# Fewer, larger loads at the end of a decode block: W1 in two, W2 in four, the last V in three

## The chip, the cores and the metric

The kernel runs on one core of a Trainium2 chip. Its engines work side by side, each through its own list of instructions in order: PE (matrix products, with its weight loads shown apart as PEld), DVE (vector operations), ACT (activation functions), POOL, and SP, which here does nothing but issue loads. Data moves between the chip's main memory and the core's on-chip memory on 16 DMA engines. The metric is the time of one execution in microseconds on the device. The kernel before takes 1312.82 us, the median of three runs (1312.65 to 1312.91).

## The reference

One token for each of two sequences (B = 2) goes through an attention block with cached keys and values, and then through a two-layer MLP. All arrays are 32-bit floats.

```python
h  = x + softmax((LN(x) @ wq) . K^T * Dh**-0.5) . V @ wo     # 32 heads, 8192 keys, Dh = 128, D = 512
y  = LN(LN(h))
h2 = h + gelu(y @ w1 + b1) @ w2 + b2                         # w1: 512 x 1792, w2: 1792 x 512
```

K and V have 2 x 32 x 8192 x 128 numbers each, 268 MB apiece, and each number is used once. W1 and W2 have 3.67 MB each.

## The kernel before

**Main loop.** A step `i` (0 to 31, `NI` = 32) is one sequence and one pair of heads. Its K tile and its V tile are 128 partitions x 128 keys x 128 numbers, 64 KB in each partition and 8.39 MB in all: partitions 0 to 63 hold one head, 64 to 127 the other. They lie in a pool of three buffers (`kv`, `BUFS = 3`), so a load waits until the tile that had its buffer three loads earlier is used up. DVE multiplies K by q in four chunks (`multiply`, L220), DVE and ACT sum over the 128 numbers (L228, L224), the maximum and the exponentials follow (`row_max`, `all_max`, `exps`), and PE multiplies the exponentials with V: `values` (L280), 32 groups `u` of four keys of each partition; each group is one product, which the trace shows as two instructions. The result lies in PSUM (`so`); ACT copies it out (`gather`, L286), and PE sums it over partitions (`head_sum`, L301, and L294 for the last two steps).

**Loads.** SP issues nearly all of them, in program order. Step 31's V, `vt[31]` (L354), is loaded in four pieces, by keys of a partition: 0-63, 64-95, 96-119 and 120-127. Behind it come four small loads of b1 and b2 (L359, L360), then W1 in four loads of 128 rows each (L415, one row of 7 KB for each partition, `c` counting the loads), then W2 in six (L419), of 4, 4, 2, 2, 1 and 1 rows of 2 KB for each partition. W1 and W2 share one tile `ws` of the pool `kv`, in the buffer that step 31's K had.

**The end, from L411 on.** Only products of step 31 and the MLP are left. PE's order there is written out by hand: `behind(last)` puts the instructions in its block after `last`. The order is: `values` of the last V for groups 0-15; `head_end` of step 30 (L294, then DVE's L423); 4 products of nothing that keep PE running (`keep_warm`, L461); groups 16-23; `into`, which starts two sums in PSUM with the residual rows (L470); 8 of `keep_warm`; groups 24-29 and 30-31; `keep_warm`; `head_end` of step 31. Group `u` reads keys 4u to 4u+3, so groups 0-15 need the first V piece, 16-23 the second, 24-29 the third, 30-31 the fourth.

Then `project` multiplies by the last rows of wo twice (L477): into `hc`, which holds h with its mean taken out, and into `po2`, which holds h + b2. `hc` has column block `n` (128 of the 512 columns of h) in partitions 32n and 32n+1. DVE copies it (L504), PE turns it (L509), and the result `cen` has column 128n + p of h in partition p. It is multiplied with W1 (L520; W1's row 128c + p lies in partition p), the variance comes from L526 and L528, then follow the scale and b1 (L536), gelu (L538, ACT), a turn in 32 x 32 blocks (L540, DVE), W2 in 14 products `t` of four blocks each (L543), a copy (L546) and the store (L548).

Of the kernel before, what the change touches and what calls it, by code (L numbers as in the profile page):

```python
# [16 lines left out]
P = 128  # L17
# [5 lines left out]
NG = 4  # L23
# [9 lines left out]
def tile_decode_block(ctx: ExitStack, tc: tile.TileContext, x, k, v, wq, wo, w1, b1, w2, b2, out):  # L33
    nc = tc.nc
    B, H, SK, DH = k.shape
# [5 lines left out]
    DC = D // P  # L41
# [19 lines left out]
    def load(src, i, parts):  # L61
        m, b = divmod(i, B)
        t = kv.tile([P, NS, DH], F32, name="kv", tag="kv")
        rows = src[b, QG * m:QG * m + QG].rearrange("h (p j) d -> (h p) j d", j=NS)
        for s0, n in parts:
            nc.sync.dma_start(t[:, s0:s0 + n], rows[:, s0:s0 + n])
        return t
# [4 lines left out]
    ident = const.tile([P, P], F32, name="ident")  # L72
# [88 lines left out]
    otl = const.tile([P, QG, B], F32, name="otl")  # L161
# [51 lines left out]
    wl = q2.rearrange("p (e n) -> p e n", e=QG)  # L213

    def multiply(i, c):
        if c == 0:
            ST[i] = work.tile([P, NS], F32, name="s", bufs=3)
        qb = qps[i // B][:, i % B, None, :].to_broadcast([P, CH, DH])
        kc = kt[i][:, c * CH:(c + 1) * CH, :]
        return nc.vector.tensor_tensor(kc, kc, qb, op=ALU.mult)  # L220

    def by_act(i, c):
        for j in range((c + 1) * CH - NACT[c], (c + 1) * CH):
            nc.scalar.activation(kt[i][:, j, :], kt[i][:, j, :], AF.Copy, accum_out=ST[i][:, j:j + 1])  # L224
# [12 lines left out]
    def all_max(i):  # L237
        gm = work.tile([1, QG], F32, name="gm")
        last = nc.vector.tensor_reduce(gm, MT.pop(i).rearrange("o (e p) -> o e p", e=QG), axis=AX.X, op=ALU.max,  # L239
                                       negate=True)  # L240
        GM[i] = psm.tile([P, 1], F32, name="sm")
        for e in range(QG):
            nc.tensor.matmul(GM[i][e * HP:(e + 1) * HP], srow, gm[:, e:e + 1], start=True, stop=True)  # L243
        return last

    def exps(i):
        m, b = divmod(i, B)
        nb = work.tile([P, 1], F32, name="nb")
        nc.scalar.activation(nb, GM.pop(i), AF.Copy)  # L249
        if b == 0:  # L250
            LT[m] = work.tile([P, B], F32, name="ls")
        s = ST.pop(i).rearrange("p (u j) -> p u j", j=4)
        for e in range(QG):
            ps = slice(e * HP, (e + 1) * HP)
            nc.scalar.activation(ptz[i % 2][ps, :, 4 * e:4 * e + 4], s[ps], AF.Exp, bias=nb[ps], scale=SCALE,  # L255
                                 accum_out=LT[m][ps, b:b + 1])
# [19 lines left out]
    def values(i, us=range(NS // 4)):  # L276
        so = so2[i % 2]
        for u in us:
            n = u % NG
            m = nc.tensor.matmul(so[32 * n:32 * n + 4 * QG], ptz[i % 2][:, u, :], vt[i][:, 4 * u:4 * u + 4, :],  # L280
                                 start=(u < NG), stop=(u >= NS // 4 - NG))
        return m
# [52 lines left out]
    def behind(m):  # L335
        return tc.issue_after(m.ins)

    def cut(n):
        return [(j * NS // n, NS // n) for j in range(n)]

    parts_of = {NI - 3: cut(2), NI - 2: cut(4), NI - 1: cut(2)}
    kt, vt = {}, {}
# [3 lines left out]
    for i in range(NI):  # L346
        m, b = divmod(i, B)
        done = i - 1
        late = i == NI - 1
        if not late:  # L350
            if i < NI - 2:
                vt[i] = load(v, i, cut(1))
        else:
            vt[i] = load(v, i, [(0, 64), (64, 32), (96, 24), (120, 8)])  # L354
            b1r = rows2[:, 0].rearrange("p r q -> p (r q)")[:, :FN]
            nc.vector.memset(b1r, 0.0)
            b2s = rows2[:B, 1].rearrange("b r q -> b (r q)")
            for e in range(B):
                nc.sync.dma_start(b1r[e::32], b1.rearrange("(n f) -> n f", n=NG))  # L359
                nc.sync.dma_start(b2s[e:e + 1], b2[None, :])  # L360
        if i > 0:
            last = all_max(done)
            exps(done)
            if not late:
                values(done)
        if i < NI - 1:
            kt[i + 1] = load(k, i + 1, parts_of.get(i + 1, cut(1)))
        if i == NI - 2:
            vt[i] = load(v, i, cut(1))
            nc.sync.dma_start(wl, wo[HL * DH:, :].rearrange("(h p) n -> p h n", p=P))  # L370
        if next_load < len(groups) and i == free_from:
            load_wo(next_load, MX[i - 1][:1, 0:1] if next_load == 0 else None)
            next_load += 1
            free_from = NI
        for c in range(NC):
            if i > 0 and c == 0:
                with behind(last):
                    mul = multiply(i, c)
            else:
                mul = multiply(i, c)  # L380
            ended = [g for g in group_end.get(done // B, ())] if done >= 0 and done % B == B - 1 else []
            with behind(mul):
                if i > 0 and c == 1:
                    inverse(done)
                if i > 0 and c == 2 and done % B == B - 1:
                    for h in range(done // B * QG, done // B * QG + QG):
                        head_out(h)
                if c == 3:
                    for g in ended:
                        turned(g)  # L390
                        free_from = i + 1
            by_act(i, c)
            if i > 0 and c == 0 and not late:
                gather(done)
            by_dve(i, c)
            if i > 0 and c == 0:
                total(done)
            if i > 0 and c == 1 and not late:
                head_sum(done)
            if c == 2:  # L400
                for g in ended:
                    turn(g)
        if b == B - 1 and m + 1 < NM:
            make_q(m + 1)
        if late:
            with behind(values(done, range(MOST))):
                row_max(i)
        else:
            row_max(i)
# [1 line left out]
    hl = NI - 1  # L411
    wt = kv.tile([P, 2, NS * DH // 2], F32, name="ws", tag="kv")
    w1t = wt[:, 0, :DC * F].rearrange("p (c f) -> p c f", c=DC)
    for c in range(DC):
        nc.sync.dma_start(w1t[:, c], w1[c * P:(c + 1) * P])  # L415
    w2v = w2.rearrange("(p t) d -> p t d", t=FT)
    w2t = wt[:, 1, :FT * D].rearrange("p (t d) -> p t d", t=FT)
    for t, n in ((0, 4), (4, 4), (8, 2), (10, 2), (12, 1), (13, 1)):
        nc.sync.dma_start(w2t[:, t:t + n, :], w2v[:, t:t + n, :])  # L419

    def head_end(i):
# [3 lines left out]
    last = all_max(hl)  # L425
# [5 lines left out]
    with behind(last):  # L431
        last = values(hl - 1, range(MOST, NS // 4))
# [9 lines left out]
    wlc = late[:, 0:QG, :]  # L442
# [9 lines left out]
    basec = late[:B, 3, :]  # L452
# [9 lines left out]
        return m  # L462


    po2 = psq.tile([P, 512], F32, name="po2", tag="qps")[:, :P]
    hc = psm.tile([P, P], F32, name="sm")

    def into(t, rows):
        for n in range(NG):
            m = nc.tensor.matmul(t[32 * n:32 * n + 32], ident[:B, :32], rows[:, n * P:(n + 1) * P],  # L470
                                 start=True, stop=False)
        return m

    def project(t, w, stop):
        for n in range(NG):
            for e in range(QG):
                m = nc.tensor.matmul(t[32 * n:32 * n + B], otl[:, e, :], w[:, e, n * P:(n + 1) * P],  # L477
                                     start=False, stop=stop and e == QG - 1)
        return m

    with behind(last):
        last = values(hl, range(NS // 8))
    with behind(last):
        head_end(hl - 1)
        last = keep_warm(WARM)
    for a, e in ((16, 24), (24, 30), (30, 32)):
        with behind(last):
            last = values(hl, range(a, e))
        if e == 24:
            with behind(last):  # L490
                into(po2, b2s)
                last = into(hc, basec)
            with behind(last):
                last = keep_warm(2 * WARM)
    SS[hl] = work.tile([P, 512], F32, name="ss", bufs=3)
# [2 lines left out]
    with behind(last):  # L498
        last = keep_warm(WARM)
    with behind(last):  # L500
        head_end(hl)
        last = project(hc, wlc, True)
    hs = const.tile([P, P], F32, name="hs")
    nc.vector.tensor_copy(hs, hc)  # L504
    with behind(last):
        last = project(po2, wl, False)
    hT = psm.tile([P, NG, 32], F32, name="sm")
    with behind(last):
        last = nc.tensor.transpose(hT.rearrange("p n r -> p (n r)"), hs, ident)  # L509
# [8 lines left out]
    for c in range(DC):  # L518
        for n in range(NG):
            last = nc.tensor.matmul(  # L520
                pf[32 * n:32 * n + B], cen[:, c, :], w1t[:, c, n * FN:(n + 1) * FN],
                start=(c == 0), stop=(c == DC - 1))
        if c == 0:
            with behind(last):
                for n in range(NG):
                    last = nc.tensor.matmul(vp[32 * n:32 * n + 32], sv, onesd, start=True, stop=True)  # L526
# [48 lines left out]
```

## Time and profile before

| | |
|---|---|
| median of the runs | 1312.82 us |
| the profiled execution | 1313.52 us, its span 1311.0 us, mean granted PE clock 0.655 |
| DVE busy | 971.8 us (74%) |
| ACT busy | 479.3 us (37%) |
| PE busy | 460.7 us (35%) |
| bytes read | 561.5 MB, mean 428 GB/s over the span |

The span runs from the first to the last instruction; the execution's own time has 2.5 us around it. The DMA engines are busy nearly the whole time: 39 of the 40 slices of the span show a DMA share of 90% or more. So the time is that of moving 561 MB, with a beginning and an end in which the engines also wait for each other. "Granted clock" is the share of full speed at which PE runs, and in this trace it is 0.5 or 1.0, switched by how busy PE has been. In a timeline, a line gives start, duration, engine, line, operation, out<-in, count, and in brackets how long the engine was idle before and what ended it. The lines of the end of the kernel stand with the prediction.

### The profile page before, as it was taken

What the parts mean: (1) busy time and instruction counts of PE and PEld (TensorE: products, weight loads), DVE (VectorE), ACT (ScalarE), POOL (GpSimd) and SP (SyncE); (2) the same over time, 40 slices, a digit from 0 to 9 for tenths busy, and PEclk for the clock granted to TensorE, in tenths of its full rate; (3) what the DMA queues carried; (4) which work ended last, traced back from release to release, by engine and by line L of the source; (5) the groups of instructions that cost most, each with busy time, mean ns of one, the idle gap of its engine ahead of it and who ended that gap; (6) DMA issues with size and microseconds to landing.
All of it is one profiled execution on the core that took longest, in us unless ns stands there. A gap on an engine that the chain in (4) does not pass through costs nothing.

```text
span 1311.0 us, 10398 instructions
## 1 busy us (share of the span) xinstructions
PE 460.7 (35%) x3265; PEld 144.4 (11%) x3265; DVE 971.8 (74%) x448; ACT 479.3 (37%) x2955; POOL 12.8 (1%) x18
## 2 busy tenths in 40 slices
PE   3034224443332434313342243424313344223537
PEld 0001001010010101001010010101001010010103
DVE  1766788767788676787776798767797677798991
ACT  0333344333344333343342344332343342444441
POOL 0000000000000000000000000000000000000000
PEclk9567556666566666657766566666667667566769
DMA  9999999999999999999999999999999999999997
GB/s 416 436 427 443 424 439 424 438 427 434 433 432 436 425 442 426 436 429 433 432 432 431 434 431 436 424 441 426 435 440 423 441 424 440 418 436 425 442 418 309
DMA packets 13470, 561.67 MB, mean 428 GB/s; under 512 B 1556, under 2 KB 1572, under 8 KB 2984
## 3 DMA queue, kind: packets, MB, share of 16 engines
q1 hardware_dynamic: 12828, 557.34, 98.6%
q0 software_dynamic: 576, 3.67, 0.7%
q8 instruction: 25, 0.41, 0.1%
q14 instruction: 29, 0.24, 0.0%
q10 hardware_dynamic: 12, 0.01, 0.0%
HBM read 561.53 MB, written 0.00 MB: 428 GB/s over the span
## 4 chain that ended last, share of the span: by engine, by line
DMA 49%; DVE 30%; PE 14%; issue 6%; ACT 1%; POOL 0%; SPq 0%; DVEq 0%; POOLq 0%
DMA kv<-in_A_k_cache_dram 44%; DVE kv L220 20%; PE so L280 10%; DVE s L228 8%; PE rowacc L332 3%; DMA kv<-in_A_v_cache_dram 3%; DMA ws<-in_B_w_dram 2%; ACT pt L255 1%; DVE orow L315 1%; PE sm L243 0%; PE sm L235 0%; DVE gm L239 0%; ACT nb L249 0%; DVE mx L232 0%; PE sm L323 0%
## 5 line engine op out<-in xcount | busy, mean ns | idle before, releaser
L220 DVE TENSOR_TENSOR kv<-kv,qps 128x4096 f32<-128x4096 f32 x128 | 560.8, 4412 | 276.8 <-DMA kv<-in_A_k_cache_dram 276.8
L224 ACT ACTIVATE kv<-kv 128x128 f32<-128x128 f32 x1376 | 403.9, 295 | 328.5 <-DVE kv L220 328.5
L228 DVE TENSOR_REDUCE s<-kv 128x20 f32<-128x2560 f32 (+2 forms) x128 | 377.7, 2973 | 0.3
L280 PE MATMUL so<-kv,pt 128*8 128x512 f32 x2048 | 288.4, 722 | 57.1 <-ACT pt L255 36.5
L224 ACT ACTIVATION_READ_ACCUMULATOR kv<-kv 128x1 f32 x1376 | 257.0, 187 | 0.0
L235 PE MATMUL sm<-ident,mx 128*1 128x128 f32 x32 | 11.0, 343 | 312.6 <-DVE mx L232 312.6
L286 ACT ACTIVATE ss<-so 128x512 f32<-128x512 f32 x31 | 18.5, 597 | 276.8 <-PE so L280 143.9
L205 PE MATMUL qps<-q,pick 2*64 2x128 f32 x128 | 16.7, 409 | 280.4 <-DVE kv L220 280.4
L280 PEld LDWEIGHTS so<-kv,pt 128*8 128x8 f32 x2048 | 59.0, 102 | 256.3 <-issue 212.9
L249 ACT ACTIVATE nb<-sm 128x1 f32<-128x1 f32 x32 | 5.5, 171 | 167.4 <-PE sm L243 167.4
L332 PE MATMUL rowacc<-wog,ot 128*2 128x512 f32 x64 | 46.7, 898 | 52.7 <-issue 27.1
L301 PE MATMUL sm<-ss,selr 128*2 128x128 f32 x480 | 55.8, 275 | 0.7 <-ACT ss L286 0.7
L205 PEld LDWEIGHTS qps<-q,pick 2*64 2x64 f32 x128 | 10.9, 202 | 294.3 <-DVE kv L220 271.8
L301 PEld LDWEIGHTS sm<-ss,selr 128*2 128x2 f32 x480 | 39.1, 85 | 13.7 <-ACT ss L286 1.7
L323 PE MATMUL sm<-ident,orow 2*128 2x2 f32 x32 | 4.5, 241 | 102.7 <-DVE orow L315 102.7
L235 PEld LDWEIGHTS sm<-ident,mx 128*1 128x1 f32 x32 | 2.5, 79 | 329.7 <-issue 284.0
L239 DVE TENSOR_REDUCE gm<-sm 1x2 f32<-1x128 f32 x32 | 8.9, 279 | 30.0 <-PE sm L235 30.0
L255 ACT ACTIVATE pt<-s,nb 64x128 f32<-64x128 f32 x64 | 25.5, 399 | 1.6 <-ACT nb L249 0.2
L332 PEld LDWEIGHTS rowacc<-wog,ot 128*2 128x2 f32 x64 | 6.5, 110 | 85.1 <-issue 59.1
L323 PEld LDWEIGHTS sm<-ident,orow 2*128 2x128 f32 x32 | 4.0, 209 | 104.8 <-issue 77.6
L243 PE MATMUL sm<-gm,srow 1*64 1x1 f32 x128 | 11.1, 237 | 11.5 <-DVE gm L239 11.5
L192 PE MATMUL so<-wqs,yT 128*2 128x512 f32 x64 | 9.8, 780 | 14.6 <-DMA wqs<-in_A_wq_dram 14.6
(104 smaller groups left out, 122.1 us busy)
## 6 DMA issues: line engine op xcount, KB each, us to landing
kv<-in_A_k_cache_dram SPq DMA_DIRECT2D x4, 4096.0 KB
kv<-in_A_k_cache_dram SPq DMA_DIRECT2D x4, 2048.0 KB, 26.0
wog<-in_A_wo_dram SPq DMA_DIRECT2D x4, 1024.0 KB, 37.5
kv<-in_A_v_cache_dram SPq DMA_DIRECT2D x1, 4096.0 KB, 35.9
ws<-in_B_w_dram SPq DMA_DIRECT2D x4, 896.0 KB, 10.8
kv<-in_A_v_cache_dram SPq DMA_DIRECT2D x1, 2048.0 KB, 40.5
ws<-in_B_w_dram SPq DMA_DIRECT2D x2, 1024.0 KB
kv<-in_A_v_cache_dram SPq DMA_DIRECT2D x1, 1536.0 KB
```

The lines of the kernel that those rows point to most:

```text
L205: nc.tensor.matmul(qps[m][e * HP:(e + 1) * HP, b], pick[32 * n:32 * n + B, b, :], q2[32 * n:32 * n + B, at + e * DH:at + (e + 1) * DH], st ...
L220: return nc.vector.tensor_tensor(kc, kc, qb, op=ALU.mult)
L224: nc.scalar.activation(kt[i][:, j, :], kt[i][:, j, :], AF.Copy, accum_out=ST[i][:, j:j + 1])
L228: return nc.vector.tensor_reduce(ST[i][:, a:e], kt[i][:, a:e, :], axis=AX.X, op=ALU.add)
L235: nc.tensor.transpose(MT[i], mx, ident)
L243: nc.tensor.matmul(GM[i][e * HP:(e + 1) * HP], srow, gm[:, e:e + 1], start=True, stop=True)
L255: nc.scalar.activation(ptz[i % 2][ps, :, 4 * e:4 * e + 4], s[ps], AF.Exp, bias=nb[ps], scale=SCALE, accum_out=LT[m][ps, b:b + 1])
L280: m = nc.tensor.matmul(so[32 * n:32 * n + 4 * QG], ptz[i % 2][:, u, :], vt[i][:, 4 * u:4 * u + 4, :], start=(u < NG), stop=(u >= NS // 4 - ...
L286: return nc.scalar.activation(SS[i], so2[i % 2], AF.Copy)
L301: nc.tensor.matmul(OP[m][:, e, :], sel_row[:, c, 4 * e + j, :], SS[i - 1 + c][:, j * DH:(j + 1) * DH], start=(c == 0 and j == 0), stop=(c ...
L315: nc.vector.tensor_scalar(orow[g % 2][:B, :r, p0:p0 + run].rearrange("b r p -> b p r"), OP[h // QG][:, h % QG, c0:c0 + run * r].rearrange( ...
L332: nc.tensor.matmul(rowacc, t[:, r, :], wo_g[g][:, r, :], start=False, stop=(g == len(groups) - 1 and r == n - 1))
```

## The change

The last V comes in three pieces, keys 0-95, 96-119 and 120-127. W1 comes in two loads. In each, a partition gets two neighbouring rows, a run of 14 KB, and partition p holds rows 4p to 4p+3 of W1 instead of rows p, 128+p, 256+p and 384+p. So that h meets the right rows, column block `n` of `hc` becomes every fourth column of h, n, n+4, n+8 and so on: PE reads `basec` and `wlc` with a step of four numbers (`every_fourth`). `po2` keeps its order (`in_order`). W2 comes in four loads, of 7, 4, 2 and 1 rows for each partition. The bytes moved, the products and the order written for PE are the same.

```diff
-            vt[i] = load(v, i, [(0, 64), (64, 32), (96, 24), (120, 8)])
+            vt[i] = load(v, i, [(0, 96), (96, 24), (120, 8)])
...
-    for c in range(DC):
-        nc.sync.dma_start(w1t[:, c], w1[c * P:(c + 1) * P])
+    w1v = w1.rearrange("(p c) f -> p c f", c=DC)
+    for c in range(0, DC, 2):
+        nc.sync.dma_start(w1t[:, c:c + 2], w1v[:, c:c + 2])
...
-    for t, n in ((0, 4), (4, 4), (8, 2), (10, 2), (12, 1), (13, 1)):
+    for t, n in ((0, 7), (7, 4), (11, 2), (13, 1)):
...
+    def in_order(w):
+        return [w[..., n * P:(n + 1) * P] for n in range(NG)]
+
+    def every_fourth(w):
+        return [w[..., n::NG] for n in range(NG)]
...
-            m = nc.tensor.matmul(t[32 * n:32 * n + 32], ident[:B, :32], rows[:, n * P:(n + 1) * P],
+            m = nc.tensor.matmul(t[32 * n:32 * n + 32], ident[:B, :32], rows[n],
...
-                m = nc.tensor.matmul(t[32 * n:32 * n + B], otl[:, e, :], w[:, e, n * P:(n + 1) * P],
+                m = nc.tensor.matmul(t[32 * n:32 * n + B], otl[:, e, :], w[n][:, e],
...
-                into(po2, b2s)
-                last = into(hc, basec)
+                into(po2, in_order(b2s))
+                last = into(hc, every_fourth(basec))
...
-        last = project(hc, wlc, True)
+        last = project(hc, every_fourth(wlc), True)
...
-        last = project(po2, wl, False)
+        last = project(po2, in_order(wl), False)
```

## The prediction

> **What bounds the kernel now.** I read the page first (span, rate by slice), then the chain of work that ended last, SP's own waits, the timeline of the last 45 us, and windows there.
>
> ```profile
> span 1311.0 us, 10398 instructions
> ...
> GB/s 416 436 427 443 424 439 424 438 427 434 433 432 436 425 442 426 436 429 433 432 432 431 434 431 436 424 441 426 435 440 423 441 424 440 418 436 425 442 418 309
> ```
>
> The loads run at 428 GB/s in the mean up to the last slice, so nothing before the last V is of interest: the change touches none of it. The chain's last four rows (start, duration):
>
> ```profile
> 1244.06 40.46 DMA kv<-in_A_v_cache_dram
> 1284.53 9.42 DMA ws<-in_B_w_dram
> 1293.97 13.18 DMA ws<-in_B_w_dram
> 1307.19 0.45 PE po L543 x8
> ```
>
> The last load, W2's row 13, lands at 1307.19, one product (0.45) follows, then copy and store, and the span ends 3.4 us after that product. SP's waits (total, times, longest):
>
> ```profile
> SPq L415 <- DMA kv<-in_A_v_cache_dram: 18.1, 4, 9.4
> SPq L419 <- DMA ws<-in_B_w_dram: 1.5, 1, 1.5
> ```
>
> W1's four loads are each issued only when a piece of the last V has landed: 1279.69 to 1289.5. Counting along SP's list, each waits for the load eight places before it; so does the last W2 load, which waits for W1's second (the chain's 1293.97). I take that as the rule: eight loads in flight.
>
> PE's side of the end:
>
> ```profile
> 1268.04 6.62 PE L280 MATMUL so<-kv,pt 128*8 128x512 f32 x48 [17.05 <-DMA kv<-in_A_v_cache_dram]
> ...
> 1279.75 3.62 PE L280 MATMUL so<-kv,pt 128*8 128x512 f32 x32 [0.67 <-DMA kv<-in_A_v_cache_dram]
> ...
> 1283.30 1.05 PE L294 MATMUL sm<-sel,ss 128*128 128x2 f32 x8
> ...
> 1284.74 1.91 PE L280 MATMUL so<-kv,pt 128*8 128x512 f32 x16
> ...
> 1286.93 1.05 PE L461 MATMUL wp<-ident 128*128 128x256 bf16 x8
> ...
> 1288.24 2.28 PE L280 MATMUL so<-kv,pt 128*8 128x512 f32 x16 [0.26 <-DMA kv<-in_A_v_cache_dram]
> ...
> 1302.64 2.59 PE L543 MATMUL po<-ws,pt 128*2 128x128 f32 x80 [0.65 <-DVE pt L540]
> 1305.89 1.06 PE L543 MATMUL po<-ws,pt 128*2 128x128 f32 x24 [0.66 <-DMA ws<-in_B_w_dram]
> 1307.19 0.40 PE L543 MATMUL po<-ws,pt 128*2 128x128 f32 x8 [0.24 <-DMA ws<-in_B_w_dram]
> ```
>
> The reader is to see that PE starts on the last V at 1279.75 and is then busy almost without a break until 1290.52: its waits for V pieces after that are 0.21, 0.26 and 0.28, together 0.75. From 1290.52 a chain of dependent steps over PE, DVE and ACT takes 12.12 us to the first L543. So **two strands arrive nearly together**: the loads at 1307.19, and PE, which ran L543 at 0.259 us per t (2.59 / 10), so 14 of them need 3.63, and with all of W2 there it would be done at 1306.27 instead of 1307.59. PE has 1.32 us to spare, no more. The granted clock (before the DMA share):
>
> ```profile
> 1260.00:1270.00 10.00, 1.96 (x12) 0.48 (x16) 10.00 (x4) 5.72 (x39) 0.00 (x0) 0.50 0.97 409
> 1270.00:1275.00 5.00, 4.67 (x40) 0.91 (x32) 4.97 (x2) 0.61 (x5) 0.00 (x0) 0.93 0.97 416
> ...
> 1280.00:1285.00 5.00, 5.00 (x48) 2.02 (x44) 1.61 (x5) 0.92 (x2) 0.00 (x0) 1.00 0.95 392
> 1285.00:1290.00 5.00, 4.74 (x48) 1.49 (x40) 0.00 (x0) 0.00 (x0) 0.00 (x0) 1.00 0.90 330
> ```
>
> After its 17 us of idleness PE began at 1268.04 at 0.5 and got 1.0 at about 1270.7 (0.93 over 5 us is 0.35 us of the half clock).
>
> **The change part by part.**
>
> *V in three pieces.* It removes one issue on SP (0.33, hidden: SP waits for lanes and buffers anyway) and 8 runs per DMA engine. It moves PE's first 16 groups: they now wait for keys 0-95, which are there when the second piece was, 1284.53, in place of 1279.6. PE starts at about 1284.65 (landing to product took 0.06 to 0.22 before), 4.9 later. Queued behind that wait, by the order written out, are head_end of step 30 (so DVE's first L423 too), all keep_warm, both `into`, the other groups and everything after. None of it can move ahead. Of the 4.9, the 0.75 of waits behind is no longer waited, since the pieces at 1288.2 and 1289.4 are long there: the values end 4.15 later, 1294.7. Less PE's spare 1.32: **+2.8** at the end.
>
> *The clock.* In the hole from 1279.07 (end of L264) to 1284.65 PE has nothing: 5.6 us. The rows show the clock falling after the bursts ending 1189.9, 1225.0 and 1246.2 at 1192.2, 1229.7 and 1250.2 (worked out from the window shares in the same way), 2.3 to 4.7 us into the idle time, so here it has fallen by the time that V comes. It comes back 2.7 (1268.0 to 1270.7), 3.3 (1240.1 to 1243.4) or 4.9 us (1211.2 to 1216.1) after a burst starts. Half of that is lost: 1.35 to 2.45; none, if it should not fall. I take 3.3 us at half, **+1.65**, the middle row. The chain behind had a half-clock stretch of its own (0.70 over 1295 to 1300, so 1294.6 to 1298.0), which cost about 1.2, most of it in W1's first block (1.68 for 8 instructions against 0.89 in the 2.67 for 24). Shifted, it can be gone or fall on two blocks: -1.2 to +0.8; I take 0.
>
> *W1 in two loads, W2 in four.* Four issues fewer on SP. With eight in flight, the places shift: b1/b2 wait for loads that landed by 1267.9 and still queue behind the last V; W1's first load waits for wl (landed 1269.96) and for step 31's K to be used up (DVE's L228 ends at 1274.97): issued at 1275.0, 4.7 earlier. W1's second waits for the first V piece (1284.5), W2's first two for the other V pieces (1288.2, 1289.4), the rest follow at once. Bytes are the same, so the gain is what the engines lose now: 392 and 330 GB/s against 428 in the two windows above is 0.42 + 1.14 = 1.56 us at most. At the least nothing, because a load lands with its slowest engine, and that one shows no gap: the pieces at 1279.6 and 1284.5 lie 4.9 apart for 2.1 MB, 427 GB/s, and from 1289.48 to 1307.19 come 7.34 MB, 414 GB/s. The difference of 414 to 427 is 0.5 us, small runs; 32 of the 80 that each DMA engine has in W1 and W2 go. I take 0.3: the last row lands at about 1306.9. With PE beginning L543 near 1308.4 all of that is **off the path, 0**; W1, complete at about 1298 as now, is not waited for either (L520 starts near 1301.7).
>
> *Every fourth column.* Four `into` products (0.42 for their 8 instructions) and eight of L477 (0.64 for 16) read with a step of 16 bytes. No product in the trace streams its moving operand so. Nearest row: weight loads of 2x128 with just that step (L181, 213 ns median) against without (L323, 219 ns): no cost. Far row: as if all 512 columns were streamed for the 128 that count, like L280's, whose instruction of 512 columns takes 0.107 where a quarter is 0.027: 0.08 for each of 16 and of 8, +1.3 and +0.6, **0 to +1.9**; a gain is excluded, as the count of products and columns stays. I take 0, the nearest row.
> The Trainium skill, "SBUF — State Buffer", section "Door 1: the DMA port swizzle", says that the memory works in 16-byte lines and that an access crossing to a new line each time pays. It gives no price; by it the sum would be on the 1.9 side, by the row on the side of 0.
>
> Sum: 2.8 + 1.65 = **+4.4** (2.8 to 6.3 with the bounds of clock and stretch that add). The profiled 1313.52 becomes 1317.9; it lies 0.70 over the median, so 1317.2 for that.
>
> **The rivals.**
> 1. *A stall in the chain goes away.* DVE's L454 (h + b2, 0.67) now stands behind L504 at 1293.26 though its inputs were there before; PE's L470 and second L477 wait for it, and so L509 starts at 1295.16 instead of about 1293.7. If the planner, with V late, puts L454 ahead of the end of the values, 1.4 goes: 1315.8. For it: DVE is idle from 1281.5 on. Against: nothing in the edit names it.
> 2. *The stepped reads cost*, as priced: +1.9, 1319.1.
> 3. *Not slower: the transfers set the end, as the chain now says.* Their fuller queue gives up to 1.56: 1311.3 to 1312.8. It decides if L543 starts no later than about 1303.3, so if PE's slip is under 0.7. Against it: the 4.15 above follows from the order of the instructions.
> 4. *Fewer loads, less fixed cost.* If each load paid a fixed time by itself, one after the other, the loads would end sooner by that time for each of the five that go. A lone one is bounded by the store: 3.0 us from its issue at 1307.98 to the end. But four of the five come behind the last V, where they are off the path; PE's strand gains by the one V load, 3.0 at most: 1314.2. The rows are against it: W1's and W2's ten loads take 17.7 us where the bytes at 427 GB/s need 17.2, so a fixed cost hides behind the neighbours.
> The Trainium skill, "DMA: Bandwidth & Descriptors", section "Anatomy of one DMA", gives 2.0 us plus the bytes at 436 GB/s for one DMA, so that by it 2.0 would go here (an estimate); for loads queued behind each other the trace disagrees.
>
> **How the numbers follow.** Forecast 0.50, at 1317.2, its own range 1315.6 to 1318.7. Rivals 1 to 4: 0.20, 0.10, 0.13, 0.03; 0.04 for what I don't see. A measurement of this kernel tells 0.2%, 2.6 us, from no change: 1310.2 to 1315.4. Slower: 0.47 of the forecast, 0.13 of rival 1, 0.10 of 2, 0.01 of the rest, 0.71. Same: 0.03 + 0.07 + 0.12 of rival 3 + 0.03 of rival 4, 0.25. Faster: 0.01 of rival 3 and 0.03 of the rest, 0.04. The range reaches down past rival 4 and up past rival 2 and leaves out rival 3 and the rest: 1313.5 to 1319.3.
>
> **What would show it.** Right: the first L280 on the last V near 1284.6, its 32 instructions taking about 5 us rather than 3.62, the clock under 1.0 there; values ending near 1296; L543 starting near 1308 and running 14 t without a wait for W2; the chain that ended last going through V, then PE and DVE, no longer through ws. W1's first issue near 1275. Wrong: L543 still waiting for ws, L477 well over 0.64, or L454 ahead of L504.

## The result, and the profile after

The changed kernel takes 1316.52 us (median of nine runs, 1315.66 to 1317.25), the kernel before 1312.95 us beside it (nine runs, 1312.65 to 1313.34). The ratio is 1.0027, with a 95% interval of 1.0019 to 1.0035: slower by 3.6 us. The profiled execution took 1316.52 us, with a span of 1314.7 us against 1311.0.

The chain of work that ended last has changed hands. These are its three largest pieces from the load of the last V on, in order of time (start, duration, what):

```profile
1243.65 40.79 DMA kv<-in_A_v_cache_dram
1284.58 5.64 PE so L280 x32
...
1307.87 3.28 PE po L551 x112
```

Before, the loads of `ws` stood there up to 1307.19. Now no load after the last V's first piece does: from 1284.58 on the chain is made of PE, DVE and ACT. SP's timeline shows W1's first load issued at 1275.49 in place of 1279.69, W2's first at 1288.16:

```profile
1275.49 9.32 SPq L416 DMA_DIRECT2D ws<-in_B_w_dram  x2
1288.16 2.54 SPq L420 DMA_DIRECT2D ws<-in_B_w_dram  x4
```

So the weights are asked for earlier, and nobody waits for them. PE's and DVE's timeline of the end (the lines of the file have moved: L462 is `keep_warm`, L478 `into`, L485 `project`, L455 h + b2, L512 the copy of `hc`, L517 the turn, L528 W1, L551 W2):

```profile
1284.58 5.64 PE L280 MATMUL so<-kv,pt 128*8 128x512 f32 x32 [5.04 <-DMA kv<-in_A_v_cache_dram]
1290.15 1.05 PE L294 MATMUL sm<-sel,ss 128*128 128x2 f32 x8
...
1291.32 0.68 DVE L455 TENSOR_TENSOR orow<-late,orow 2x512 f32<-2x512 f32 x1
1291.59 1.90 PE L280 MATMUL so<-kv,pt 128*8 128x512 f32 x16
1293.42 0.64 PE L478 MATMUL sm<-late,ident 2*32 2x128 f32 x8
1293.99 1.05 PE L462 MATMUL wp<-ident 128*128 128x256 bf16 x8
1294.97 1.02 PE L280 MATMUL so<-kv,pt 128*8 128x512 f32 x2
1295.92 0.42 PE L478 MATMUL po<-orow,ident 2*32 2x128 f32 x8
1296.27 1.90 PE L280 MATMUL so<-kv,pt 128*8 128x512 f32 x14
...
1299.98 1.12 PE L485 MATMUL sm<-late,otl 128*2 128x128 f32 x16 [0.25 <-DVE otl L424]
...
1301.19 0.29 DVE L512 COPY hs<-sm 128x128 f32<-128x128 f32 x1 [1.26 <-PE sm L485]
1301.54 0.33 PE L517 MATMUL sm<-ident,hs 128*128 128x128 f32 x1
...
1302.12 0.93 PE L528 MATMUL so<-ws,cen 128*2 128x448 f32 x8 [0.26 <-DVE cen L519]
...
1307.87 3.24 PE L551 MATMUL po<-ws,pt 128*2 128x128 f32 x112 [0.64 <-DVE pt L548]
```

The first group of 32 instructions starts 4.8 us later and takes 5.64 us instead of 3.62. W2's 112 instructions run through in one piece; before, they were cut by waits for `ws`: four on the weight loads, 2.2 us together, and two of them, 0.9 together, on the products. The windows (length, busy times, granted clock, DMA share, GB/s) show the clock:

```profile
1280.00:1285.00 5.00, 0.42 (x4) 0.15 (x8) 1.91 (x4) 1.38 (x2) 0.00 (x0) 0.69 0.92 388
1285.00:1290.00 5.00, 5.00 (x32) 0.88 (x24) 0.00 (x0) 0.00 (x0) 0.00 (x0) 0.63 1.00 418
```

PE has 0.42 us of work in the first window and is busy all through the second, at 0.63 of full speed. Both windows were at 1.00 before. If the clock is taken as 0.5 or 1.0, these shares give a fall at 1281.9 and a return at 1288.7.

Reading the two timelines along PE's strand, start to start, gives the whole of the span's 3.7:

| stretch of the strand | before | after | difference |
|---|---|---|---|
| first product on the last V, start | 1279.75 | 1284.58 | +4.83 |
| from there to `head_sum` of step 30 | 3.55 | 5.57 | +2.02 |
| to the start of `hc` | 3.28 | 3.27 | 0.0 |
| start of `hc`, to `keep_warm` | 0.35 | 0.57 | +0.22 |
| `keep_warm`, to group 24 | 1.31 | 0.98 | -0.33 |
| groups 24 to 31 | 2.21 | 3.13 | +0.92 |
| then to the projection | 1.87 | 1.88 | 0.0 |
| projection into `hc`, to its copy | 0.74 | 1.21 | +0.47 |
| copy of `hc` to the turn | 2.10 | 0.35 | -1.75 |
| turn, to W1 | 0.74 | 0.58 | -0.16 |
| W1 to W2 | 6.74 | 5.75 | -0.99 |
| W2 to the last copy | 5.02 | 3.30 | -1.72 |
| last copy to the end of the span | 3.34 | 3.53 | +0.19 |

### The profile page after: what moved, and what is told of

It is laid out like the page before. It is cut to its first block, busy times and chain, and to the rows that moved or that the text cites. A ratio compares the mean times of both kernels' runs of the same rounds, so it can differ in the third digit from the quotient of the medians.

```text
span 1314.7 us, 10392 instructions
## 1 busy us (share of the span) xinstructions
PE 451.9 (34%) x3265; PEld 143.6 (11%) x3265; DVE 971.8 (74%) x448; ACT 479.6 (36%) x2955; POOL 12.8 (1%) x18
## 4 chain that ended last, share of the span: by engine, by line
DMA 48%; DVE 30%; PE 15%; issue 6%; ACT 1%; POOL 0%; SPq 0%; DVEq 0%; POOLq 0%
DMA kv<-in_A_k_cache_dram 45%; DVE kv L220 20%; PE so L280 10%; DVE s L228 8%; DMA kv<-in_A_v_cache_dram 3%; PE rowacc L332 3%; ACT pt L255 1%; DVE orow L315 1%; PE sm L243 0%; PE sm L235 0%; DVE gm L239 0%; PE po L551 0%; PE so L528 0%; ACT nb L249 0%; DVE mx L232 0%
## 5 line engine op out<-in xcount | busy, mean ns | idle before, releaser
L332 PE MATMUL rowacc<-wog,ot 128*2 128x512 f32 x64 | 43.9, 849 | 52.7 <-issue 27.1
```

The lines of the kernel that those rows point to most:

```text
L332: nc.tensor.matmul(rowacc, t[:, r, :], wo_g[g][:, r, :], start=False, stop=(g == len(groups) - 1 and r == n - 1))
```

## The experiments

The theory: the bigger first piece of V makes PE start late and at half clock, PE's spare time and the waits and the stall that went pay for a part of it, the stepped reads add 0.7, and the loads of W1 and W2 do not matter. The rivals: the W loads cost; the stepped reads are the larger part; the loads still set the end.

**V in three pieces alone** (the kernel before with one line):

```diff
-            vt[i] = load(v, i, [(0, 64), (64, 32), (96, 24), (120, 8)])
+            vt[i] = load(v, i, [(0, 96), (96, 24), (120, 8)])
```

> The kernel before with one edit: the last V in three pieces. If the bigger first piece makes PE late (the theory), nearly all of the change's +3.6 us is here: the first product on the last V at about 1284.6 after a hole of 5 us, the half clock there, DVE's h + b2 ahead of the copy of hc. Only the stepped reads are missing, which took 0.7 longer in the changed kernel: 2.9 over before, about 1315.9. If the loads of W1 and W2 are what costs, no change: 1312.9. If the stepped reads are the larger part, under 1.5 over before.

Measured: 1315.91 us, before 1313.14; ratio 1.0022 (1.0013 to 1.0032), 2.8 over. The timeline has all that the changed kernel's has, except for the two rows of stepped reads: the start of `hc` takes 0.42 here and the projection 0.64:

```profile
1284.48 5.49 PE L280 MATMUL so<-kv,pt 128*8 128x512 f32 x32 [5.19 <-DMA kv<-in_A_v_cache_dram]
...
1293.17 0.42 PE L470 MATMUL sm<-late,ident 2*32 2x128 f32 x8
...
1299.52 0.64 PE L477 MATMUL sm<-late,otl 128*2 128x128 f32 x16 [0.25 <-DVE otl L423]
```

One edit to one load accounts for about three quarters of the loss. DVE's h + b2 also stands ahead of the copy of `hc` here, so that move comes with V, not with W1 or W2.

**W1, W2 and every fourth column alone** (the changed kernel with that line put back to four pieces).

> The changed kernel with the last V in four pieces again, so W1 in two, W2 in four and every fourth column alone. If V's first piece is the cause, PE starts on the last V at 1279.75 again; the stepped reads take 0.7 of the 1.3 that PE has to spare, and the last row of W2 lands 0.3 earlier: -0.5 to +0.1 against before, 1312.5 to 1313.0. If the W loads or the reads cost beyond what PE has to spare, 1 us or more over before.

Measured: 1313.04 us, before 1313.14; ratio 0.9999 (0.9990 to 1.0008). No difference. The end of its chain reads like that of the kernel before, with the last row landing 0.34 earlier, and the loads set the end again:

```profile
1289.68 16.39 DMA ws<-in_B_w_dram
...
1306.85 0.45 PE po L551 x8
```

It has two waits that were not there before: for W1's second load, which now brings two row blocks at once, and some 0.2 us for W2's first, which brings seven rows (the blocks that it multiplies were ready at 1302.20):

```profile
1298.07 1.68 PE L528 MATMUL so<-ws,cen 128*2 128x448 f32 x16 [0.51 <-DMA ws<-in_B_w_dram]
...
1302.46 1.71 PE L551 MATMUL po<-ws,pt 128*2 128x128 f32 x56 [0.85 <-DMA ws<-in_B_w_dram]
```

Both lie ahead of waits for later rows of W2 and cost nothing here. The row of W1's first 8 instructions is of use further down: they take 0.94 here, with the last V still in four pieces, where they took 1.68 in the kernel before.

```profile
1295.82 0.94 PE L528 MATMUL so<-ws,cen 128*2 128x448 f32 x8 [0.26 <-DVE cen L519]
```

So the W half of the change neither gains nor loses.

**V in two pieces**, the suspected cost doubled (the changed kernel with `[(0, 120), (120, 8)]`).

> The changed kernel with the last V in two pieces, keys 0-119 and 120-127: the suspected cost doubled. The first piece is then there at 1288.15 instead of 1284.5. If the first piece sets PE's start and PE the end, 3.6 more than the changed kernel: 7.2 over before, about 1320.1. If something else sets the end, the same as the changed kernel, 1316.5.

Measured: 1318.69 us, before 1313.14; ratio 1.0044 (1.0029 to 1.0059), 5.5 over where the changed kernel is 3.6 over. PE did start 3.5 later, at 1288.04, and the end moved with it, but by 1.3 less (spans of 1316.9 and 1314.7 us). The timeline shows where that went:

```profile
1288.04 5.74 PE L280 MATMUL so<-kv,pt 128*8 128x512 f32 x32 [8.45 <-DMA kv<-in_A_v_cache_dram]
...
1296.98 0.42 PE L478 MATMUL po<-orow,ident 2*32 2x128 f32 x8
1297.23 0.63 PE L478 MATMUL sm<-late,ident 2*32 2x128 f32 x8
...
1298.77 1.90 PE L280 MATMUL so<-kv,pt 128*8 128x512 f32 x16
```

In the changed kernel the start of `po2` (L478, `po`) stands in the middle of the last 16 instructions on V, and these take 3.13 with it, from 1294.97 to 1298.10. Here it stands beside the start of `hc`, and they take 1.83, start to start. The planner, which orders what `behind` leaves open, had placed DVE's h + b2 earlier in this kernel (1282.28), and PE's order is another too; that the one led to the other is not shown. My number missed because I had shifted the strand as a block.

**DVE puts the columns in order**, so that PE reads without a step:

```diff
-        nc.vector.tensor_scalar(wlc[:, e, :], wl[:, e, :], wmean[:, e:e + 1], None, op0=ALU.subtract)
+        nc.vector.tensor_scalar(wlc[:, e, :].rearrange("p (n j) -> p n j", n=NG),
+                                wl[:, e, :].rearrange("p (j n) -> p n j", n=NG),
+                                wmean[:, e:e + 1], None, op0=ALU.subtract)
...  (basec in the same way; PE then takes both with in_order)
```

> The changed kernel, but DVE writes the centred rows of wo and of the residual with the columns already in blocks of every fourth, so that PE reads them without a step; DVE has no other work there (1278 to 1284). If the step costs PE 0.22 in the sum's start and 0.47 in the projection, as the two traces differ, this gives 0.7 back: about 1315.8, L485's 16 instructions at 0.64 again. If those differences come from something else (what stands beside them), the same as the changed kernel, 1316.5.

Measured: 1315.85 us, before 1313.14; ratio 1.0020 (1.0011 to 1.0029), 2.7 over before where the changed kernel is 3.6 over. The projection and the start of `hc` (0.42) are short again, and nothing else on the strand is of another length but the first group (5.11; it varies, see below):

```profile
1292.80 0.42 PE L481 MATMUL sm<-late,ident 2*32 2x128 f32 x8
...
1299.14 0.64 PE L488 MATMUL sm<-late,otl 128*2 128x128 f32 x16 [0.25 <-DVE otl L424]
```

The reordering itself takes DVE 1.26 us for the two instructions on `wlc` instead of 0.88, and 0.70 for the one on `basec` instead of 0.47, in a stretch where DVE has nothing else to do. The row, 1.12 to 0.64 with the step and without, shows the stepped read's price; the 0.9 between the medians agrees with it, though the two intervals overlap.

**The hole filled** (the changed kernel):

```diff
+    with behind(last):
+        last = keep_warm(40)
     with behind(last):
         last = values(hl, range(NS // 8))
```

> The changed kernel with 40 products of nothing (L461's kind, about 0.12 us each, 4.8 us) in the hole before the last V. If the half clock after the hole costs what the first group of 32 instructions took longer (5.64 against 3.62), 2.0 us of the changed kernel's 3.6 go: about 1314.6, 1.6 over before, and the group takes 3.62 again. If the group is slow for another reason, the same as the changed kernel, 1316.5.

Measured: 1314.52 us (1314.30 to 1315.03), before 1313.01; ratio 1.0012 (1.0003 to 1.0021), 1.5 over. The first group is back at its length, and the clock is 1.00 in both windows:

```profile
1284.38 3.62 PE L280 MATMUL so<-kv,pt 128*8 128x512 f32 x32 [1.03 <-DMA kv<-in_A_v_cache_dram]
...
1280.00:1285.00 5.00, 3.97 (x39) 3.02 (x41) 2.00 (x4) 0.90 (x2) 0.00 (x0) 1.00 0.91 384
1285.00:1290.00 5.00, 5.00 (x48) 2.01 (x44) 0.76 (x2) 0.00 (x0) 0.00 (x0) 1.00 1.02 420
```

So 2.0 of the 3.6 were the half clock, and products of nothing in idle time bought it back here.

**W1 and W2 alone, columns ordered by DVE** (V in four pieces, no stepped reads).

> W1 in two and W2 in four with the last V in four pieces, and DVE writing the columns in order. PE's strand is 0.7 shorter than with the W change alone, but the loads end the kernel there (the last row of W2 landed at 1306.85), so by the theory nothing changes: 1312.6 to 1313.1. If PE's strand still sets the end with the W change alone, 0.7 less: 1312.3.

Measured: 1312.89 us, before 1313.01; ratio 0.9998 (0.9989 to 1.0007). PE's strand is shorter, and the end stays: the last product waits for W2's last row, as in the kernel before.

```profile
1306.30 0.62 PE po L554 x16
1306.94 0.44 PE po L554 x8
```

**The start of `po2` ahead of the products of nothing** (the changed kernel):

```diff
-                into(po2, in_order(b2s))
                 last = into(hc, every_fourth(basec))
+            with behind(last):
+                last = into(po2, in_order(b2s))
```

> The changed kernel with the start of po2 written behind the start of hc and ahead of the 8 products of nothing, instead of wherever the planner puts it. It now stands between the second and the third of the last 16 instructions on V, where those took 3.2 us in place of 2.05. If PE loses time by that change of operands, 0.8 is gained (1.1 less its own 0.3): about 1315.7. If it is hidden, 1316.5.

Measured: 1315.62 us, before 1313.01; ratio 1.0019 (1.0009 to 1.0028), 2.6 over before, so 0.9 or 1.0 less than the changed kernel, though the two intervals overlap here as well. The last 16 instructions on V are one piece again, 1.83 us from start to start where the changed kernel has 3.13; this row shows the price. This profile also had the longest first group of all, 6.37 us, so its own span of 1314.5 says little; the median of eleven runs does.

```profile
1284.70 6.37 PE L280 MATMUL so<-kv,pt 128*8 128x512 f32 x32 [4.30 <-DMA kv<-in_A_v_cache_dram]
...
1296.05 1.90 PE L280 MATMUL so<-kv,pt 128*8 128x512 f32 x16
```

**The three together**: hole filled, columns ordered by DVE, `po2` started early, and V still in three pieces.

> The changed kernel with the three together: hole filled, columns ordered by DVE, po2 started ahead of the products of nothing. If the late start is paid for by the stall that went and by PE's spare time, and the rest of the change's cost is these three terms, 2.0 + 0.7 + 0.8 of the 3.6 go: 1313.0, like before, V still coming in three pieces. If a part of the cost is elsewhere, 1 us or more over before is left.

Measured: 1312.77 us, before 1313.01; ratio 0.9997 (0.9988 to 1.0006). With the three terms gone nothing is left of the loss, though PE still starts on the last V at 1284.75: PE's W2 products end at 1307.5, as before, and the chain ends on them, without a wait for `ws`:

```profile
1284.75 3.62 PE so L280 x32
1304.26 3.28 PE po L557 x112
```

It has the lowest median of all kernels run, but no kernel here beats the one before by more than the measurement can tell. Where V comes in four pieces, the last row of W2 ends the kernel, and the change brought that forward by only 0.3 us.

## Why the prediction was right

The time came out at 1316.52, 0.7 under the forecast of 1317.2 and inside its own range; against the runs of before beside it, +3.6 where +4.4 was forecast. By its steps:

- *What bounds the kernel*: right. Two strands end nearly together, loads and PE, and PE had little to spare. V alone and W alone show each side.
- *V in three pieces, +2.8*: right in its parts. The start moved by 4.83 (4.9), the first wait on a V piece was not on the path after all (from `keep_warm` to group 16 it is 0.53 before and after), the other two were (0.33, and 0.38 as 2.21 against the 1.83 of the kernel with `po2` started early). Together that is 0.71 of the 0.75. PE's spare was 1.72 rather than 1.32, because W2's 14 products run at 0.231 us each when nothing is waited for; the 0.259 I used came from a row that already held some of the waiting.
- *The clock, +1.65*: measured 2.02, from the profiles, and 2.0 from filling the hole. The half clock lay on PE's work for 4.1 us (1284.6 to 1288.7) where 3.3 was taken.
- *The half-clock stretch behind, taken as 0*: it went. W1's first 8 instructions took 0.93 instead of 1.68, and W1 to W2 is 0.99 shorter; with the 0.16 from the turn to W1 that is 1.15. -1.2 was the lower bound. It need not be the change that took it away: with W1, W2 and every fourth column alone, V in four pieces, the profile has no such stretch either (0.94, granted clock 1.00 over 1295 to 1300). There is one profile of the kernel before, so whether the stretch is in each of its executions is open; where it is not, PE has more to spare there than the 1.72.
- *Fewer W loads, off the path, 0*: right. They moved the last landing by 0.34 and 0.25 in the two profiles with V early (0.3 estimated) and the time by nothing. That the slowest DMA engine has no gap was argued from rates; no view here separates the engines. That W1's second load would be waited for was not foreseen (0.51 and 0.96 us in those two kernels); it hid behind W2.
- *Every fourth column, 0*: the term that was mis-sized. It costs 0.22 and 0.47, together 0.69, so rival 2 came in part, at a third of its price. The nearest row, a weight load with the same step, was the wrong neighbour: a weight load is not a streamed operand. The Trainium skill, "SBUF — State Buffer", section "Door 1: the DMA port swizzle", has accesses that reach a new 16-byte line each time pay a penalty; that is the side on which the runs came out (1.12 us against 0.64 for the same 16 instructions), and they add the price. The same note gives "4 fp32" as how far one can stride for free; if that is to include a step of exactly four numbers, these runs decide against it.
- *Rival 1, a stall goes away*: it happened, beside the forecast rather than in place of it. The planner put h + b2 ahead of the copy of `hc`, and 1.75 went there, a little more than the 1.4 forecast. But it also put the start of `po2` into the middle of V's last products. Groups 24 to 31 took 0.92 longer in spite of the 0.38 of waiting that they no longer had, so 1.3 was given back, and the rival's net was 0.45.
- *Rivals 3 and 4*: no. The W change alone is within 0.1 us of before, and V with one load less is slower. The section that rival 4 names in the Trainium skill has its 2.0 us from DMAs issued by GpSimd; SP issues these loads, and no run here isolates one of them.

Of the signs named beforehand, most of those for being right came: the start at 1284.58, the first group at 5.64 with the clock under 1.0, the chain on V and then PE, W1's first load at 1275.49. But two of the three for being wrong came as well: the projection at 1.12 and h + b2 ahead of the copy of `hc`. And the last product on V ended at 1298.2, not near 1296; that W2's products still began at 1307.87, near the 1308 forecast, is because the stall and the half-clock stretch behind were gone.

So the errors on the span were 0.69 for the stepped reads, 0.37 for the clock after the hole and 0.19 behind the last copy on the one side, and 1.15 for the stretch behind, 0.45 for the stall and 0.40 for the spare on the other; they left 0.75. The mechanism was right; the closeness of the sum is in part luck.

## What to carry to other kernels

Where loads and an engine end nearly together, the size of the first piece of the last tile is what that engine's start hangs on: here, with the DMA engines busy nearly all the time, fewer and larger loads brought the last landing 0.3 us forward and saved nothing, while the engine paid the wait for the bigger piece and, after a hole of some 5 us, the half clock too. Before moving a start, count what the other strand has to spare, and put products of nothing into a hole that can't be avoided. An edit to one load can also change where a planner puts work two engines away, so read the order of instructions beside the times.

## What the runs showed that was not expected

- A moving operand read with a step of 16 bytes made 16 matmul instructions of 128 columns take 1.12 us instead of 0.64, and the 8 of `into`, with two partitions, 0.64 instead of 0.42. Putting the columns in order on DVE cost 0.38 and 0.23 us more there, off the path.
- A few small products in the middle of a run of large ones on PE cost far more than their own time: two large instructions, 1294.97 to 1295.92, where two take 0.21 in a run, then 0.35 for the small ones. The kernel before has the same at 1275.70, where `row_max` and `all_max` put small products on both sides of two large ones, and they take 0.96 to the next start. Why the two take so long is open; that it costs is shown by the kernel that moves them (0.9 less).
- The length of the half clock after the hole changes from profile to profile, and with it the first group of 32 instructions, which always takes 3.62 us without a hole. The changed kernel's runs spread over 1.6 us, those with the hole filled over 0.7. These are the granted clocks of three windows and the time at half clock that they give:

| kernel | 1280 to 1285 | 1285 to 1290 | 1290 to 1295 | at half clock, us | first group, us |
|---|---|---|---|---|---|
| changed | 0.69 | 0.63 | 1.00 | 6.8 | 5.64 |
| V in three alone | 0.65 | 0.67 | 1.00 | 6.8 | 5.49 |
| V in two | 0.71 | 0.50 | 0.76 | 10.3 | 5.74 |
| DVE puts the columns in order | 0.91 | 0.75 | 1.00 | 3.4 | 5.11 |
| `po2` started early | 0.85 | 0.50 | 0.97 | 6.8 | 6.37 |

Each length is one, two or three times 3.4 us. What the group loses is half of the part that falls behind its own start. The Trainium skill, "TensorE: Matmul & The Clock Gate", section "What's actually happening", says that the clock is decided in free-running windows of 3413 ns; the trace agrees: the lengths are one to three such windows, and they lie differently to the start of the group in each profile.
